# Keys of the windowed block in rows of 16 KB: four heads to a load, and column groups exchanged behind the transposes

## The chip, the cores and the metric

The kernel runs on one core of a Trainium2 chip. The metric is the time of one execution in microseconds (us): the median of the runs, 440.17 us for the kernel before (three runs, 440.09 to 440.18). Beside the runs there is one profiled execution, whose rows are used below.

## The reference, cut to what matters

Two attention blocks, A and B, each decode one token for four sequences. Both have 32 query heads over 8 key and value heads, 8192 cached tokens and 128 numbers to a head. Block A looks at all cached tokens, block B at the last 2048 alone.

```
q = (x @ wq)                                  # x: [4, 1, 512], 32 heads of 128
k, v = cache (A: all 8192 tokens; B: the last W = 2048)   # [4, 8, 8192, 128], bf16
scores = q . k * 128 ** -0.5                  # four query heads share one kv head
o = softmax(scores) @ v
out = concat(o_A @ wo_A, o_B @ wo_B)          # [4, 1, 1024]
```

All of the caches that are looked at are read once: 2 x 67.1 MB for A, 2 x 16.8 MB for B. With the weights the core reads 184.56 MB.

## The kernel before, in words

**Units.** The work is cut into 20 units (the list `units`). Units 0 to 3 belong to B (`P == 1`): one sequence each, all eight heads, 2048 tokens. Units 4 to 19 belong to A (`P == 0`): one sequence and one pair of heads (`gp`) each, 8192 tokens. Each unit has 4 MB of keys and 4 MB of values. `K_sb` and `V_sb` have two slots each, taken in turn by even and odd units (`slot = u % 2`). A slot is 128 partitions of 128 tokens (`NT`) of 256 bytes.

**How a load lies.** `kv_load` (L712) issues the loads, all of them from SyncE's queue (SP). For A, one DMA fills a slot: partition p gets 128 tokens in a row, 32 KB, so that the first 64 partitions hold one head and the last 64 the other. The source pattern is one run of 128 rows. For B, four DMAs (`NSEG`) of 1 MB fill a slot, each with one pair of heads in rows of 32 tokens, 8 KB; the source is walked as 64 rows, 2 heads, 8 KB, and so the two heads alternate from partition to partition.

**Keys.** A unit's keys are transposed in 16 steps (`pe_T`, L270): each step makes four fp32 transposes (two tokens each, bf16 pairs taken as fp32) into one of four PSUM banks (`KT`). VectorE (even steps, L287) or ScalarE (odd steps, L288) copies the bank into `KT_sb`. `pe_S` (L300) then makes eight score matmuls against `RQc`, into `SA` for the first half of the tokens and `SB` for the second (L310). The scores' partition is the column of the transposed key, and it has to agree with the partition of the values in `V_sb`, for `pe_PV` (L317) multiplies the weights with `V_sb` (L326).

**Masks.** A score tile has two heads on its partitions, and for each column one of them counts. `MASK[0]` (A: halves of the partitions) is written by GpSimd's memsets. `MASK[1]` (B: alternating partitions) is made by writing `MK` and spreading it with two DMAs from GpSimd's queue (L563); the first `M1m` waits for them (`("mk", 1)`).

**Order.** TensorE, VectorE and ScalarE run hardware loops over turns of two units, TensorE over all ten turns, with the same instructions in each. In unit u, TensorE does the 16 transposing steps with the scores three steps behind (`LA = 3`), then the values of unit u - 1. SP's queue is in the order of the program: both `wq`, then K of unit 0, and from there K of unit u, V of unit u - 1, and every second unit a piece of `wo`. Each DMA waits until its buffer is free: B's keys by parts (part q waits for transposing step 4q + 3 of unit u - 2), A's keys for the last transposing step of unit u - 2 (u < 6) or for the output of unit u - 3 (`otr`), V for the output of unit u - 2 before it in its slot. The last unit's loads are cut finer (K in two, V in five), and at the end come eight small loads of `wo` (`Wl_sb`).

Of the kernel before, what the change touches and what calls it, by code (L numbers as in the profile page):

```python
# [7 lines left out]
F32 = mybir.dt.float32  # L8
I32 = mybir.dt.int32
ACTF = mybir.ActivationFunctionType  # L10
# [4 lines left out]
def bass_concat_heads__gqa_block_cached__sliding_block_cached__decode_kernel(  # L15
# [34 lines left out]
    NKT = 4  # L50
# [2 lines left out]
    NBK = 4  # L53
    NFILL = 3
    NTH = NT // 2
    X = [A_x, B_x]
    KC = [A_k_cache, B_k_cache]
    VC = [A_v_cache, B_v_cache]
# [13 lines left out]
    with ExitStack() as es:  # L72
        block = es.enter_context(nc.Block())

        def sb(name, shape, dt):
            return es.enter_context(nc.sbuf_tensor(name, shape, dt))
# [4 lines left out]
        def sm(name):  # L81
# [14 lines left out]
        MK = sb("MK", [128, NSEG * C], F32)  # L96
# [28 lines left out]

        names = ["k0", "k1", "kh", "v0", "v1", "vl0", "vl1", "vl2", "vl3", "vl4", "wl0", "wl1", "wl2", "wl3", "wl4", "wl5", "wl6", "wl7", "x0", "x1", "w0", "w1", "wo",
                 "out0", "out1", "out2", "Tq", "Td", "Ta", "S", "PV", "Ed", "Ea", "Eq", "vs", "sub", "exp", "otr", "otp",
                 "ocp", "Ef", "fin0", "fin1", "ar1", "SM", "msk", "pset", "setup", "pm0", "pm1", "oc", "ocB", "mk0", "mk", "mka", "perm", "rq"]
        sems = {n: sm("s_" + n) for n in names}

        K_sbf = K_sb.bitcast(F32)
# [123 lines left out]
        def pe_filler(n):  # L255
# [8 lines left out]
                return ins  # L264
            op("pe", fn, waits=[("F", p) if jobs[p]["turn"] is not None else None])

        def pe_T(u, k):
            eng = "dve" if k % 2 == 0 else "act"
            idx = tjob_idx[(u, k)] = new_job("T", eng)
            tj = u * NJ + k  # L270
            bkf = kbank(idx)
            bk = bkf.bitcast(BF16)
            slot = u % 2

            def fn(pe):
                ins = None
                for pi in range(4):
                    t0 = k * 8 + 2 * pi
                    ins = pe.transpose(out=bkf[:, pi * 128:(pi + 1) * 128],  # L279
                                       in_=K_sbf[:, slot, t0:t0 + 2, :].rearrange("p t d -> p (t d)"),  # L280
                                       identity=identf[:, :])
                return ins
            op("pe", fn, waits=[("K", u) if k == 0 else ("KH", u) if k == NJ // 2 and u % 2 == 1 else None, bankfree(idx)], inc=("T", idx))

            def efn(e):
                if eng == "dve":
                    return e.tensor_copy(out=KT_sb.bitcast(I32)[:, tj % NKT, :], in_=bkf.bitcast(I32)[:, :])  # L287
                return e.activation(out=KT_sb[:, tj % NKT, :], in_=bk[:, :], func=ACTF.Copy)  # L288
            return dict(eng=eng, fn=efn, waits=[("T", idx)], inc=("E", idx))

        def pool_rq(u):
# [8 lines left out]
        def pe_S(u, k):  # L300
            tj = u * NJ + k
            stb = SA[u % 2] if k < NJ // 2 else SB
            ktv = KT_sb[:, tj % NKT, :].rearrange("p (i k e) -> p i k e", i=4, e=2)

            def fn(pe):
                ins = None
                for pi in range(4):
                    t = k * 8 + 2 * pi
# [109 lines left out]
        def dve_addmask(u):  # L418
            n, P = ncol(u), units[u]["P"]

            def fn(dve):
                return dve.tensor_tensor(out=M1m[:, 0:n], in0=M1[:, 0:n] if P == 1 else M1c[:, :], in1=MASK[P][:, 0:n], op=AluOpType.add)  # L422
            return dict(eng="dve", fn=fn, waits=[("max", u, 1) if P == 1 else ("maxc", u)] + ([("mk", 1), ("mka",)] if u == 0 else []), inc=("pm", u, 0))

        def pool_ar1(u):
            n = ncol(u)
# [81 lines left out]
            return dict(eng="pool", fn=lambda pool: pool.tensor_copy(out=OTp[:, :, :], in_=OT_sb[:, P, q, :, :]), waits=w, inc=("otp", tn))  # L508

        def pool_mask0(pool):  # L510
            mkv = MK[:, :].rearrange("p (g s h) -> p g s h", g=NSEG, s=2)
            pool.memset(mkv[0:64, :, 0, :], 0.0)
            pool.memset(mkv[0:64, :, 1, :], -BIG)
            pool.memset(mkv[64:128, :, 0, :], -BIG)
            return pool.memset(mkv[64:128, :, 1, :], 0.0)
        op("pool", pool_mask0, inc=("mk0",))

        def pool_mask1(pool):
# [4 lines left out]
        op("pool", pool_mask1, inc=("mka",))  # L523

        def pool_setup0(pool):
            pool.memset(dummy[:, :], 0.0)
# [8 lines left out]
        op("pool", pool_setup0, waits=[("mk0",), ("mka",)], inc=("pset",))  # L535
# [21 lines left out]
        for sh in range(2):  # L557
            m0 = MASK[1][:, :]
            pstm = m0.ap[0][0]
            dst_ap = bass.AP(tensor=m0.tensor, offset=m0.offset + sh * pstm, ap=[[2 * pstm, 64], [1, NSEG * C]])  # L560

            def mfn(pool, dst_ap=dst_ap, sh=sh):
                return pool.dma_start(out=dst_ap, in_=MK[64 * sh:64 * sh + 64, :])  # L563
            op("pool", mfn, waits=[("mk0",)], inc=("mk", sh))

        def dma(dst, src):
            def fn(e):
                return e.dma_start(out=dst, in_=src)  # L568
            return fn
# [140 lines left out]
        def kv_load(kind, u):  # L710
            un = units[u]
            cache = (KC if kind == "K" else VC)[un["P"]]  # L712
            buf = K_sb if kind == "K" else V_sb
            slot = u % 2
            if kind == "K" and slot == 1 and u < L:
                op("sp", lambda sp: sp.sem_inc(sems["kh"], 16), bump=(sems["kh"], 16, ("KH", u)))
            if un["P"] == 1:
                for q in range(NSEG):
                    base = cache[un["b"], 2 * q, SK - W:SK, :]
                    src = bass.AP(tensor=base.tensor, offset=base.offset, ap=[[TS * DH, 64], [SK * DH, 2], [1, TS * DH]])  # L720
                    if kind == "K":
                        w = [("T", tjob_idx[(u - 2, 4 * q + 3)])] if u >= 2 else []
                    else:
                        w = [("otr", u - 2)] if u >= 2 else [("T", tjob_idx[(1, 1)])] if u else [("T", qp_idx[(1, NQP - 1)])]
                    op("sp", dma(buf[:, slot, q * TS:(q + 1) * TS, :], src), waits=w, inc=(kind if q == NSEG - 1 else kind + "h", u, q))
# [12 lines left out]
            sem = sem_of((kind, u))  # L738
            op("sp", lambda sp: sp.sem_inc(sem, 48), waits=w, bump=(sem, 48, None))
# [28 lines left out]

        def full(key):
            if key[0] in ("K", "V") and len(key) == 2:  # L770
                return (key[0], key[1], NSEG - 1 if units[key[1]]["P"] == 1 else 0)
# [163 lines left out]
```

## Time and profile before

| what | value |
|---|---|
| median of the runs | 440.17 us |
| profiled execution: time, span | 439.76 us, 437.9 us |
| TensorE busy | 363.9 us, 83% of the span |
| VectorE, ScalarE, GpSimd busy | 209.5, 193.3, 29.1 us |
| DMA queue of SP | 12400 packets, 184.56 MB, 99.2% of 16 engines' span |
| HBM read over the span | 421 GB/s |
| mean granted TensorE clock | 0.969 |
| key copies: VectorE L287, ScalarE L288 | 690 ns, 1025 ns each, 160 of each |

The span is the time between the first and the last record of the core; 1.9 us of the profiled execution's time lie around it, and it is 0.4 us under the median. A DMA is issued by an engine's queue, and its rows are moved as packets by the core's 16 DMA engines; the profile counts the packets by queue and gives the mean share of the 16 engines that were busy. KB is 1024 bytes, MB a million.

### The profile page before, as it was taken

To read this page: it belongs to the slowest core of one execution; us is meant where nothing else is said; L and a number is where in the kernel's file an instruction comes from. 1 tells how busy PE (TensorE), PEld (TensorE's weight loads), DVE (VectorE), ACT (ScalarE), POOL (GpSimd) and SP (SyncE) were. 2 spreads that over 40 slices of the span, in tenths; PEclk is the share of its full clock that TensorE was granted. 3 is DMA by queue.
4 is the path that set the end of the run, shared out by engine and by line. 5 is a ranking of instruction groups with operands and counts; after the bars stand their busy time and mean duration, and the time that the engine had idled before them with its cause. 6 is when DMAs were issued, how large, how long until landed. Compare 5 with 4: busy or idle time off the path is not lost.

```text
span 437.9 us, 15510 instructions
## 1 busy us (share of the span) xinstructions
PE 363.9 (83%) x7174; PEld 336.5 (77%) x7184; DVE 209.5 (48%) x404; ACT 193.3 (44%) x217; POOL 29.1 (7%) x96
## 2 busy tenths in 40 slices
PE   0078898998998959896989598969878895989986
PEld 0068897997997959795979588968868795979975
DVE  0004455664565634463456247625644563556641
ACT  1033473563653625372635264534534361635630
POOL 7110000000000000000000000000100000000000
PEclk9999999999999997999899699989998999999999
DMA  8999999999999999999999999999999999999996
GB/s 336 431 412 418 419 419 419 421 445 406 450 431 431 417 445 431 434 428 431 434 434 428 432 434 431 428 434 431 406 456 431 431 428 434 431 431 410 446 407 253
DMA packets 12500, 184.75 MB, mean 422 GB/s; under 512 B 1428, under 2 KB 2504, under 8 KB 2760
## 3 DMA queue, kind: packets, MB, share of 16 engines
q1 hardware_dynamic: 12400, 184.56, 99.2%
q8 instruction: 8, 0.13, 0.1%
q14 instruction: 4, 0.03, 0.0%
q0 software_dynamic: 64, 0.02, 0.0%
q10 hardware_dynamic: 24, 0.01, 0.0%
HBM read 184.56 MB, written 0.01 MB: 421 GB/s over the span
## 4 chain that ended last, share of the span: by engine, by line
PE 51%; DMA 43%; issue 2%; DVE 1%; SPq 1%; PEld 1%; PEldq 0%
DMA K_sb<-in_A_k_cache_dram 29%; PE KT L279 25%; PE OT L326 10%; DMA K_sb<-in_B_k_cache_dram 7%; DMA V_sb<-in_A_v_cache_dram 7%; PE SB L310 4%; PE SA L310 4%; PE KT L384 4%; SPq L568 1%; PE SA L338 1%; DVE oacc L392 1%; PE KT L326 1%; PEld OT L326 1%; PE KT L262 0%; DVE OS L489 0%
## 5 line engine op out<-in xcount | busy, mean ns | idle before, releaser
L279 PE MATMUL KT<-identf,K_sb 128*128 128x128 f32 x1280 | 206.2, 294 | 44.0 <-DMA K_sb<-in_A_k_cache_dram 33.0
L288 ACT ACTIVATE KT_sb<-KT 128x1024 bf16<-128x1024 bf16 x160 | 163.4, 1025 | 121.1 <-PE KT L279 121.1
L279 PEld LDWEIGHTS KT<-identf,K_sb 128*128 128x128 f32 x1280 | 146.2, 148 | 49.4 <-DMA K_sb<-in_A_k_cache_dram 34.2
L287 DVE COPY KT_sb<-KT 128x512 int32<-128x512 int32 x160 | 110.5, 690 | 131.2 <-PE KT L279 129.9
L326 PE MATMUL OT<-PT,V_sb 128*128 128x64 bf16 x2560 | 78.1, 193 | 2.5 <-issue 1.4
L326 PEld LDWEIGHTS OT<-PT,V_sb 128*128 128x128 bf16 x2560 | 75.9, 98 | 2.7 <-issue 1.5
L457 ACT ACTIVATE PT<-Dt 128x512 bf16<-128x512 f32 x40 | 24.6, 632 | 84.1 <-DVE Dt L446 84.1
L310 PEld LDWEIGHTS SA<-RQc,KT_sb 128*128 128x128 bf16 x1280 | 56.7, 98 | 2.3
L310 PEld LDWEIGHTS SB<-RQc,KT_sb 128*128 128x128 bf16 x1280 | 51.1, 97 | 7.9 <-issue 4.4
L310 PE MATMUL SA<-RQc,KT_sb 128*128 128x16 bf16 x1280 | 56.2, 170 | 0.0
L310 PE MATMUL SB<-RQc,KT_sb 128*128 128x16 bf16 x1280 | 52.8, 170 | 0.0
L408 DVE TENSOR_REDUCE M<-SB 128x8 f32<-128x512 f32 (+1 forms) x20 | 13.8, 692 | 49.9 <-PE SB L310 49.9
L429 POOL PARTITION_ALL_REDUCE MB<-M1m x20 | 7.7, 387 | 333.3 <-DVE M1m L422 333.3
L384 PE MATMUL KT<-Wo_sb,OL 128*4 128x512 bf16 x80 | 18.9, 379 | 0.0
L200 PE MATMUL KT<-ident,x_sb 4*128 4x4 bf16 x8 | 0.6, 170 | 21.1 <-POOL identf L540 21.1
L200 PEld LDWEIGHTS KT<-ident,x_sb 4*128 4x128 bf16 x8 | 0.4, 113 | 21.3 <-issue 21.3
L464 DVE TENSOR_REDUCE LB<-SA 128x8 f32<-128x512 f32 (+1 forms) x20 | 13.7, 684 | 2.8 <-PE SA L338 2.8
L446 DVE TENSOR_TENSOR Dt<-SA,MBm 128x512 f32<-128x512 f32 x20 | 13.8, 692 | 0.7
L355 DVE TENSOR_TENSOR ORx<-KT,MSK 32x1024 bf16<-32x1024 bf16 x10 | 12.1, 1211 | 3.7 <-PE KT L350 3.7
L408 DVE TENSOR_REDUCE M<-SA 128x8 f32<-128x512 f32 (+1 forms) x20 | 13.6, 681 | 0.0
L446 DVE TENSOR_TENSOR Dt<-SB,MBm 128x512 f32<-128x512 f32 x20 | 13.6, 681 | 0.0
L338 PE MATMUL SA<-PT,onesb 128*128 128x128 bf16 x168 | 12.7, 218 | 0.0
(74 smaller groups left out, 119.7 us busy)
## 6 DMA issues: line engine op xcount, KB each, us to landing
K_sb<-in_A_k_cache_dram SPq DMA_DIRECT2D x15, 4096.0 KB, 22.6
V_sb<-in_A_v_cache_dram SPq DMA_DIRECT2D x15, 4096.0 KB, 30.6
K_sb<-in_B_k_cache_dram SPq DMA_DIRECT2D x16, 1024.0 KB, 22.0
V_sb<-in_B_v_cache_dram SPq DMA_DIRECT2D x16, 1024.0 KB, 18.4
V_sb<-in_B_wq_dram SPq DMA_DIRECT2D x1, 4096.0 KB, 12.5
V_sb<-in_A_wq_dram SPq DMA_DIRECT2D x1, 4096.0 KB, 22.0
Wo_sb<-in_B_wo_dram SPq DMA_DIRECT2D x4, 1024.0 KB, 11.9
K_sb<-in_A_k_cache_dram SPq DMA_DIRECT2D x2, 2048.0 KB, 18.9
```

The lines of the kernel that those rows point to most:

```text
L279: ins = pe.transpose(out=bkf[:, pi * 128:(pi + 1) * 128], in_=K_sbf[:, slot, t0:t0 + 2, :].rearrange("p t d -> p (t d)"), identity=identf[ ...
L287: return e.tensor_copy(out=KT_sb.bitcast(I32)[:, tj % NKT, :], in_=bkf.bitcast(I32)[:, :])
L288: return e.activation(out=KT_sb[:, tj % NKT, :], in_=bk[:, :], func=ACTF.Copy)
L310: ins = pe.matmul(out=stb[:, t % NTH * C:(t % NTH + 2) * C], lhsT=ktv[:, pi, :, e], rhs=RQc[:, u % 2, t // TS, e, :], start=(e == 0), stop ...
L326: ins = pe.matmul(out=otb[:, s * NW:s * NW + w], lhsT=V_sb[:, slot, t, :], rhs=PT[:, slot, t * C:t * C + w], start=(j == 0), stop=(j == n ...
L338: ins = pe.matmul(out=SA[u % 2][:, s * NM:(s + 1) * NM], lhsT=onesb[:, :], rhs=PT[:, u % 2, c0:c0 + NM], start=(i == 0), stop=(i == n - 1))
L355: return dve.tensor_tensor(out=ORx[:, :, :, :], in0=bk[0:NR, 0:128].rearrange("p (i o r) -> p r o i", o=1, r=C).broadcast_to([NR, C, C, 12 ...
L384: ins = pe.matmul(out=bk[0:Bn, 0:D], lhsT=OL[:, i, :], rhs=Wo_sb[:, i, :], start=(i == 0), stop=(i == C - 1))
L408: return dve.tensor_reduce(out=M1[:, h * n:(h + 1) * n].rearrange("p (s h) -> p s h", h=C), in_=bank[:, :].rearrange("p (s j h) -> p s h j ...
L446: return dve.tensor_tensor(out=Dt[:, h * NTH * C:(h + 1) * NTH * C].rearrange("p (s j h) -> p s j h", s=Sh, h=C), in0=bank[:, :].rearrange ...
L457: return act.activation(out=PT[:, u % 2, a:b], in_=Dt[:, a:b], func=ACTF.Exp, scale=scale)
L464: return dve.tensor_reduce(out=LB[:, 0:n].rearrange("p (s h) -> p s h", h=C), in_=SA[u % 2][:, 0:NSEG * NM].rearrange("p (s j h) -> p s h ...
```

## The change

- **B's keys.** Two DMAs of 2 MB fill a slot instead of four of 1 MB (`NPART["K"] = 2`). A part holds four heads; a row is 64 tokens, 16 KB. The source is walked as 4 heads, 32 rows, 16 KB. Part q waits for transposing step 8q + 7 of unit u - 2.
- **B's values.** Still four DMAs of 1 MB in 8 KB rows; the source is now walked as 2 heads, 64 rows, so the heads lie in halves of the partitions, as in A.
- **A's keys.** Same bytes and row size; the source is now walked as 2, 64, 32 KB: partitions 0 to 63 get the even rows, 64 to 127 the odd ones.
- **Transposes.** All units take other tokens in a step (`tok0`: two from each half of a half slot's segments), and the 128 columns of a transpose are written to PSUM with a step of two fp32 words, which puts A's rows back in order.
- **Copies.** For B the copies out of the bank exchange column groups, so that each score tile holds two heads. VectorE's copy keeps its size with other strides; ScalarE's becomes two of half the size. For A they stay.
- **Masks.** `MASK[1]` now has the halves too and is written by memsets; `MK`, its two DMAs and the wait for them go.

In the program as built, the number of instructions on TensorE, VectorE and GpSimd's computing ones is unchanged; ScalarE has 32 copies more, and SP issues eight loads fewer.

```diff
+    NPART = {"K": 2, "V": NSEG}
...
+        def tok0(k, pi):
+            return NTH * (k // (NJ // 2)) + TS * (pi // 2) + 4 * (k % (NJ // 2)) + 2 * (pi % 2)
+
         def pe_T(u, k):
...
-                    t0 = k * 8 + 2 * pi
-                    ins = pe.transpose(out=bkf[:, pi * 128:(pi + 1) * 128],
+                    t0 = tok0(k, pi)
+                    ins = pe.transpose(out=bkf[:, :].rearrange("p (a j x b) -> p a j b x", a=2, b=2, j=2)[:, pi // 2, pi % 2, :, :],
...
                 if eng == "dve":
-                    return e.tensor_copy(out=KT_sb.bitcast(I32)[:, tj % NKT, :], in_=bkf.bitcast(I32)[:, :])
-                return e.activation(out=KT_sb[:, tj % NKT, :], in_=bk[:, :], func=ACTF.Copy)
+                    dst, sr = KT_sb.bitcast(I32)[:, tj % NKT, :], bkf.bitcast(I32)[:, :]
+                    if units[u]["P"] == 1:
+                        dst, sr = dst.rearrange("p (b y a) -> p b y a", b=2, a=2), sr.rearrange("p (a y b) -> p b y a", a=2, b=2)
+                    return e.tensor_copy(out=dst, in_=sr)
+                dst, sr = KT_sb[:, tj % NKT, :], bk[:, :]
+                if units[u]["P"] == 1:
+                    dst, sr = dst.rearrange("p (b y a e) -> p b y a e", b=2, a=2, e=2), sr.rearrange("p (a y b e) -> p b y a e", a=2, b=2, e=2)
+                    for b in range(2):
+                        ins = e.activation(out=dst[:, b, :, :, :], in_=sr[:, b, :, :, :], func=ACTF.Copy)
+                    return ins
+                return e.activation(out=dst, in_=sr, func=ACTF.Copy)
...
-            mkv = MK[:, :].rearrange("p (g s h) -> p g s h", g=NSEG, s=2)
+            mkv = MASK[1][:, :].rearrange("p (g s h) -> p g s h", g=NSEG, s=2)
...
-                return pool.dma_start(out=dst_ap, in_=MK[64 * sh:64 * sh + 64, :])
-            op("pool", mfn, waits=[("mk0",)], inc=("mk", sh))
...
             if un["P"] == 1:
-                for q in range(NSEG):
-                    base = cache[un["b"], 2 * q, SK - W:SK, :]
-                    src = bass.AP(tensor=base.tensor, offset=base.offset, ap=[[TS * DH, 64], [SK * DH, 2], [1, TS * DH]])
+                base = cache[un["b"], 0, SK - W:SK, :]
+                hw = SK * DH
+                for q in range(NPART[kind]):
                     if kind == "K":
-                        w = [("T", tjob_idx[(u - 2, 4 * q + 3)])] if u >= 2 else []
+                        w = [("T", tjob_idx[(u - 2, 8 * q + 7)])] if u >= 2 else []
+                        ap = [[hw, 4], [2 * TS * DH, 32], [1, 2 * TS * DH]]
+                        dst = buf[:, slot, q * NTH:(q + 1) * NTH, :]
                     else:
...
+                        ap = [[hw, 2], [TS * DH, 64], [1, TS * DH]]
+                        dst = buf[:, slot, q * TS:(q + 1) * TS, :]
+                    src = bass.AP(tensor=base.tensor, offset=base.offset + q * (HKV // NPART[kind]) * hw, ap=ap)
...
-            src = bass.AP(tensor=base.tensor, offset=base.offset, ap=[[NT * DH, 128], [1, NT * DH]])
+            src = bass.AP(tensor=base.tensor, offset=base.offset, ap=[[NT * DH, 2], [2 * NT * DH, 64], [1, NT * DH]] if kind == "K" else [[NT * DH, 128], [1, NT * DH]])
...
             if kind == "K" and u == L:
...
-                    src = bass.AP(tensor=base.tensor, offset=base.offset + t0 * DH, ap=[[NT * DH, 128], [1, NTH * DH]])
+                    src = bass.AP(tensor=base.tensor, offset=base.offset + t0 * DH, ap=[[NT * DH, 2], [2 * NT * DH, 64], [1, NTH * DH]])
```

More of the change, by code (lines that the diff above doesn't have):

```diff
@@ L95, in bass_concat_heads__gqa_block_cached__sliding_block_cached__decode_kernel @@
         permE = sb("permE", [128, 2, 2, 64], BF16)
-        MK = sb("MK", [128, NSEG * C], F32)
         MASK = [sb("MASKA", [128, C], F32), sb("MASKB", [128, NSEG * C], F32)]
@@ L127, in bass_concat_heads__gqa_block_cached__sliding_block_cached__decode_kernel @@
                  "out0", "out1", "out2", "Tq", "Td", "Ta", "S", "PV", "Ed", "Ea", "Eq", "vs", "sub", "exp", "otr", "otp",
-                 "ocp", "Ef", "fin0", "fin1", "ar1", "SM", "msk", "pset", "setup", "pm0", "pm1", "oc", "ocB", "mk0", "mk", "mka", "perm", "rq"]
+                 "ocp", "Ef", "fin0", "fin1", "ar1", "SM", "msk", "pset", "setup", "pm0", "pm1", "oc", "ocB", "mk0", "mka", "perm", "rq"]
         sems = {n: sm("s_" + n) for n in names}
@@ L307, in fn @@
                 for pi in range(4):
-                    t = k * 8 + 2 * pi
+                    t = tok0(k, pi)
                     for e in range(2):
@@ L422, in fn @@
                 return dve.tensor_tensor(out=M1m[:, 0:n], in0=M1[:, 0:n] if P == 1 else M1c[:, :], in1=MASK[P][:, 0:n], op=AluOpType.add)
-            return dict(eng="dve", fn=fn, waits=[("max", u, 1) if P == 1 else ("maxc", u)] + ([("mk", 1), ("mka",)] if u == 0 else []), inc=("pm", u, 0))
+            return dict(eng="dve", fn=fn, waits=[("max", u, 1) if P == 1 else ("maxc", u)] + ([("mka",)] if u == 0 else []), inc=("pm", u, 0))
         def pool_ar1(u):
@@ L522, in pool_mask1 @@
             return pool.memset(MASK[0][64:128, REP:C], 0.0)
-        op("pool", pool_mask1, inc=("mka",))
+        op("pool", pool_mask1, waits=[("mk0",)], inc=("mka",))
         def pool_setup0(pool):
@@ L534, in pool_setup0 @@
             return pool.memset(Wo_sb[:, :, :], 0.0)
-        op("pool", pool_setup0, waits=[("mk0",), ("mka",)], inc=("pset",))
+        op("pool", pool_setup0, waits=[("mka",)], inc=("pset",))
         def pool_setup1(pool):
@@ L556, in bass_concat_heads__gqa_block_cached__sliding_block_cached__decode_kernel @@
         op("dve", dve_msk, waits=[("setup",)], inc=("msk",))
[L557 to L562, printed above, removed]
-                return pool.dma_start(out=dst_ap, in_=MK[64 * sh:64 * sh + 64, :])
-            op("pool", mfn, waits=[("mk0",)], inc=("mk", sh))
         def dma(dst, src):
@@ L717, in kv_load @@
             if un["P"] == 1:
-                for q in range(NSEG):
-                    base = cache[un["b"], 2 * q, SK - W:SK, :]
-                    src = bass.AP(tensor=base.tensor, offset=base.offset, ap=[[TS * DH, 64], [SK * DH, 2], [1, TS * DH]])
+                base = cache[un["b"], 0, SK - W:SK, :]
+                hw = SK * DH
+                for q in range(NPART[kind]):
                     if kind == "K":
-                        w = [("T", tjob_idx[(u - 2, 4 * q + 3)])] if u >= 2 else []
+                        w = [("T", tjob_idx[(u - 2, 8 * q + 7)])] if u >= 2 else []
+                        ap = [[hw, 4], [2 * TS * DH, 32], [1, 2 * TS * DH]]
+                        dst = buf[:, slot, q * NTH:(q + 1) * NTH, :]
                     else:
                         w = [("otr", u - 2)] if u >= 2 else [("T", tjob_idx[(1, 1)])] if u else [("T", qp_idx[(1, NQP - 1)])]
-                    op("sp", dma(buf[:, slot, q * TS:(q + 1) * TS, :], src), waits=w, inc=(kind if q == NSEG - 1 else kind + "h", u, q))
+                        ap = [[hw, 2], [TS * DH, 64], [1, TS * DH]]
+                        dst = buf[:, slot, q * TS:(q + 1) * TS, :]
+                    src = bass.AP(tensor=base.tensor, offset=base.offset + q * (HKV // NPART[kind]) * hw, ap=ap)
+                    op("sp", dma(dst, src), waits=w, inc=(kind if q == NPART[kind] - 1 else kind + "h", u, q))
                 return
@@ L736, in kv_load @@
                 return
-            src = bass.AP(tensor=base.tensor, offset=base.offset, ap=[[NT * DH, 128], [1, NT * DH]])
+            src = bass.AP(tensor=base.tensor, offset=base.offset, ap=[[NT * DH, 2], [2 * NT * DH, 64], [1, NT * DH]] if kind == "K" else [[NT * DH, 128], [1, NT * DH]])
             sem = sem_of((kind, u))
-            op("sp", lambda sp: sp.sem_inc(sem, 48), waits=w, bump=(sem, 48, None))
+            bump = 16 * (NPART[kind] - 1)
+            op("sp", lambda sp: sp.sem_inc(sem, bump), waits=w, bump=(sem, bump, None))
             if kind == "K" and u == L:
@@ L770, in full @@
             if key[0] in ("K", "V") and len(key) == 2:
-                return (key[0], key[1], NSEG - 1 if units[key[1]]["P"] == 1 else 0)
+                return (key[0], key[1], NPART[key[0]] - 1 if units[key[1]]["P"] == 1 else 0)
             if key[0] == "F":
```

## The prediction

> **What bounds the kernel now.** I read the page's slices first, then the DMA queues and the issues, then the waits and a table of windows.
>
> ```profile
> PE   0078898998998959896989598969878895989986
> DMA  8999999999999999999999999999999999999996
> GB/s 336 431 412 418 419 419 419 421 445 406 450 431 431 417 445 431 434 428 431 434 434 428 432 434 431 428 434 431 406 456 431 431 428 434 431 431 410 446 407 253
> ```
>
> The DMA row stands at 9 from the second slice to the last but one; TensorE dips where it waits. The windows give the rates by stage:
>
> ```profile
> 44.00:55.00 11.00, 9.58 (x236) 9.10 (x236) 5.11 (x9) 4.89 (x6) 0.70 (x2) 1.00 1.01 419
> 230.00:270.00 40.00, 33.73 (x652) 31.35 (x652) 20.26 (x40) 17.53 (x20) 1.81 (x7) 0.91 1.00 431
> ```
>
> B's 8 KB rows run at 419 GB/s over 16 engines, 26.2 GB/s an engine; A's 32 KB rows at 431, 26.9 an engine. The last two columns are the DMA share and GB/s: all sixteen engines are busy in both, so the engines are the bound. TensorE's waits confirm it for the A stage:
>
> ```profile
> PEld KT L279 <- DMA K_sb<-in_A_k_cache_dram: 34.2, 10, 5.4
> ```
>
> A unit takes 8.39 MB / 431 GB/s = 19.5 us to load; TensorE needs about 17.5 (two units from 89.45 to 124.40 us in its timeline).
>
> The next rows decide my forecast. They are the queues of SP (q1) and ScalarE (q10) and the issues on them:
>
> ```profile
> q1 hardware_dynamic: 12400, 184.56, 99.2%
> ...
> q10 hardware_dynamic: 24, 0.01, 0.0%
> ```
>
> ```profile
> K_sb<-in_A_k_cache_dram SPq DMA_DIRECT2D x15, 4096.0 KB, 22.6
> V_sb<-in_A_v_cache_dram SPq DMA_DIRECT2D x15, 4096.0 KB, 30.6
> K_sb<-in_B_k_cache_dram SPq DMA_DIRECT2D x16, 1024.0 KB, 22.0
> V_sb<-in_B_v_cache_dram SPq DMA_DIRECT2D x16, 1024.0 KB, 18.4
> ...
> x_sb<-in_B_x_dram ACTq DMA_DIRECT2D x1, 4.0 KB
> x_sb<-in_A_x_dram ACTq DMA_DIRECT2D x1, 4.0 KB
> ...
> out_dram<-osb ACTq DMA_DIRECT2D x1, 2.0 KB
> ```
>
> Count packets. q10 carried three DMAs of four rows: 12 row packets. It shows 24, so each DMA left four more, one completion for each engine that served it. SP issued 88 DMAs: 86 of 128 rows and two of four. Rows: 86 x 128 + 8 = 11016; 12400 - 11016 = 1384 = 86 x 16 + 2 x 4. So a large DMA was served by 16 engines and one whose pattern starts with a count of 4 by four. Of the large ones, B's sources start with a count of 64 (64, 2, 8 KB) and all others with 128.
>
> **The change: the loads.** The new sources start with other counts: 4 for B's keys (4, 32, 16 KB), 2 for B's values (2, 64, 8 KB), 2 for A's keys (2, 64, 32 KB). If the engines that serve a DMA follow the first count of its source, as for the four-row DMAs, B's keys run on four engines, B's values and A's keys on two. If they follow the number of rows, all stay on sixteen. The trace has no long DMA with a small first count, so these are the two ends. A second hint: the three-level sources of B are not treated as a plain run of 128 rows when they are issued:
>
> ```profile
> 55.68 2.48 SPq L568 DMA_DIRECT2D V_sb<-in_B_v_cache_dram  x4
> ...
> 124.76 0.33 SPq L568 DMA_DIRECT2D K_sb<-in_A_k_cache_dram  x1
> ```
>
> 0.62 us an issue for three levels against 0.33 for two: the queue works on the levels, not on a merged list of rows. I take the first end: the only rows with a first count under sixteen got exactly that many engines.
>
> [...]
>
> **The sum at that end.** The four engines of q10's DMAs are not named in the trace; I assume that each DMA starts from the same first engine, so that two engines get a share of everything. Their bytes, each:
> - A's keys: 15 x 4096 KB + 2 x 2048 KB = 67.11 MB on two: 33.55 MB
> - B's values: 16.78 MB on two: 8.39 MB
> - B's keys: 16.78 MB on four: 4.19 MB
> - all else (V of A, `wq`, `wo`): 184.56 - 100.66 = 83.9 MB on sixteen: 5.24 MB
>
> Together 51.38 MB, against 184.56 / 16 = 11.53 MB now. At stage rates: 33.55 / 26.98 (mean of the six 40 us windows of the A stage, 431.7 GB/s) = 1243.7 us; 8.39 / 26.2 = 320.2; 4.19 at 26.6, midway since 16 KB rows lie between, 157.7; 5.24, nine tenths in 32 KB rows, 194.9. Sum 1916.5. By q1's row instead (99.2% of 437.9 us for 11.53 MB, 37.66 us/MB) it is 1935. I take the middle, 1926. No row tells the price of an engine when fourteen others idle; the page's slices bound it. At 450 GB/s / 16 = 28.1 an engine it is 1827, at 406 / 16 = 25.4 it is 2025.
>
> Do the two engines ever run dry? SP's order keeps them fed. K of unit u waits for the output of unit u - 3, which comes some 17.5 us after K of unit u - 2 landed; K of unit u - 1 is then queued already and takes 4096 KB / 2 / 26.98 = 78 us. In the B stage the shortest cover is K of unit 2: it waits for step 7 of unit 0, while K of unit 1 (39 us on four engines) and V of unit 0 (80 us on two) are queued ahead. So they do not run dry.
>
> Ends: the first window's DMA share of 0.84 over 11 us is 1.8 us of start; after the last wait for `Wl_sb` (435.4 us) 2.5 us remain. Span 1926 + 4.3 = 1930; 1.9 us lie around it (439.76 against 437.9) and the median is 0.4 above the profiled execution: 1933 us.
>
> **The other edits, hidden under these loads.** A unit of A then lasts 78 + 9.7 (V) + 1.2 (`wo`) = 89 us with 17.5 us of TensorE work.
> - ScalarE's copies in B: two of 512 elements by L457's 632 ns, 1264 instead of 1025, eight a unit: +1.9 us on 9.5 busy. VectorE's strided copies: L408 reads PSUM with a stride at 692 ns, as fast as the straight copy's 690: nothing.
> - Strided transposes: 1280 of 294 ns with no strided write in the trace; between nothing and a doubling. Each unit has 71 us of cover.
> - Coarser waits of B's key parts, four steps later (2.7 us): queued behind 39 us.
> - Eight issues and two mask DMAs fewer; the mask wait was not among the listed waits. Nothing.
>
> If the sixteen engines stayed, the cover is what TensorE has now, 2.0 us a unit in A (19.5 - 17.5), and in B SP's lead of more than 5 us.
>
> **Rivals.**
> - *All sixteen engines stay* (the other side). Then only row size counts: B's keys, 16.78 MB at 419 GB/s, 40.0 us now; in 16 KB rows at 425 (midway), 39.5; eight completions and 64 mask packets fewer add perhaps 0.2. About -0.8 us: 439.4, on the edge of 0.2% (0.88 us), which is about what a measurement of this kernel can tell from no change. For it: four heads and two halves still make 128 rows, and B's (64, 2) source got 16. Against: q10's packets. It decides if q1 counts 16 completions for each new load. Chance 0.08.
> - *The engines are few but taken in turn.* Each DMA gets a fresh pair, and two K loads run side by side. A K slot is then refilled in 78 + 17.5 us, two slots side by side: 48 us a unit, 16 units 764; about 100 before them and 25 after: 890 us. For it: nothing names the engines. Against: nothing in the queue rows shows a rotation. Chance 0.03.
> - *Sixteen engines, but TensorE becomes the bound.* The transposes write to PSUM with a gap. In the chain four take 0.49 us, 123 ns each; 64 a unit. From 31 ns more on each, the 2.0 us of slack are gone; doubled, a unit takes 25.4 and 16 units add 94 us: 533 us. Chance 0.03. [...]
>
> **How the numbers follow.** Few engines, the same ones: 0.86, 1933 us, between 1834 and 2032 by the slices' rates (1827 and 2025 plus 6.6). That holds more than eight in ten, so it is the range. Slower 0.86 + 0.03 + 0.03 = 0.92; the sixteen-engine rival is split between faster and same, 0.04 each.
>
> **What would show it.** q1 at 9992 rows (78 x 128 + 8) plus completions: 8 x 4 + 16 x 2 + 17 x 2 + 37 x 16 + 2 x 4 = 698, together 10690 packets; with sixteen engines 9992 + 78 x 16 + 8 = 11248. A DMA share near 434 / 1930, 0.22, and 96 GB/s. About 155 us from issue to landing for A's keys (two K loads and a V, less the 17.5 us until the issue). TensorE waiting for A's keys some 70 us a unit. ScalarE's halves at 632 ns, transposes at 294 ns or more, both without effect. The prediction is wrong if the DMA row stays at 9, or if the bytes spread over changing engines, which a share well over 0.22 would show.

## The result and the profile after

The changed kernel takes 2119.99 us (median of six runs, 2107.65 to 2147.59), the kernel before 440.0 us beside it. The ratio is 4.812, with an interval of 4.790 to 4.833. The forecast was 1933 us with a range of 1834 to 2032: slower, as forecast, for the reason that was forecast, but 187 us more, and outside the range. The profiled execution took 2107.65 us, with a span of 2105.8 us.

First the queues of the changed kernel (queue, packets, MB, share of 16 engines) and the line on memory under them:

```profile
q1 hardware_dynamic: 10690, 184.56, 25.8%
...
q10 hardware_dynamic: 24, 0.01, 0.0%
...
HBM read 184.56 MB, written 0.01 MB: 88 GB/s over the span
```

10690 is to the packet the number that stands in the prediction for two, two and four engines, and the shares of busy engines agree: 0.25 of the sixteen from 30 to 40 us, where B's keys load, and 0.12 from 1060 to 1090 us, where A's keys load alone (the windows are below). But the share is 25.8% where 22% was forecast, and the rate 88 GB/s where it was 96. The prediction had named a share well over 0.22 as a sign of changing engines; it does not mean that here, as the packets show below. Put together, an engine that is busy moves 88 / (0.258 x 16) = 21.3 GB/s; before it was 421 / (0.992 x 16) = 26.5. The engines are few, and those that work are slow as well.

The slices of the span for the changed kernel:

```profile
PE   1321201210210302122021303030303022030313
DMA  5212121111141314132512313311413131322162
GB/s 195 91 74 71 73 71 70 53 55 53 54 114 54 134 54 110 59 126 94 136 50 68 116 54 134 118 49 55 126 54 113 71 117 58 108 119 69 51 162 76
```

Many slices of the A stage read 53 to 55 GB/s: two engines at 27 each, the full rate (A's 431 GB/s before are 26.9 an engine). The slices between them, over 100 GB/s, are those with a load on sixteen engines. The first slices after `wq`, where B's keys and values are loaded on four and two engines, stand at 70 to 91.

The costliest groups (count, then busy us and mean ns of one, then idle time before them):

```profile
L282 PE MATMUL KT<-identf,K_sb 128*128 128x128 f32 x1280 | 234.2, 325 | 1415.2 <-DMA K_sb<-in_A_k_cache_dram 1267.9
...
L293 DVE COPY KT_sb<-KT 128x512 int32<-128x512 int32 x160 | 110.5, 690 | 1528.8 <-PE KT L282 1527.5
...
L298 ACT ACTIVATE KT_sb<-KT 128x512 bf16<-128x512 bf16 x64 | 34.7, 594 | 302.0 <-PE KT L282 302.0
```

TensorE's transposes wait 1267.9 us for A's keys. Its list of waits has 17 of them (total us, count, longest us):

```profile
PE KT L282 <- DMA K_sb<-in_A_k_cache_dram: 1267.9, 17, 87.2
...
PE OT L338 <- DMA V_sb<-in_B_v_cache_dram: 262.3, 4, 71.6
...
PE KT L282 <- DMA K_sb<-in_B_k_cache_dram: 147.1, 4, 56.9
```

A wait for A's keys takes 1267.9 / 17 = 74.6 us in the mean (the longest 87.2), where some 70 were forecast for a unit. The profile page gives no time from issue to landing for these loads, so the forecast 155 us stay unchecked. The copies are as cheap as was said: VectorE's stay at 690 ns, ScalarE's halves take 594, and both wait for TensorE nearly all the time.

### The profile page after: what moved, and what is told of

It is laid out like the page before. It is cut to its first block, busy times and chain, and to the rows that moved or that the text cites. A ratio compares the mean times of both kernels' runs of the same rounds, so it can differ in the third digit from the quotient of the medians.

```text
span 2105.8 us, 15531 instructions
## 1 busy us (share of the span) xinstructions
PE 400.9 (19%) x7174; PEld 373.1 (18%) x7184; DVE 209.6 (10%) x404; ACT 195.7 (9%) x249; POOL 27.8 (1%) x94
## 3 DMA queue, kind: packets, MB, share of 16 engines
q1 hardware_dynamic: 10690, 184.56, 25.8%
## 4 chain that ended last, share of the span: by engine, by line
another core or an unknown queue 80%; PE 19%; issue 1%; POOL 0%; ACT 0%; DVE 0%; POOLq 0%
PE KT L282 10%; PE OT L338 4%; PE SB L322 1%; PE SA L322 1%; PE KT L396 1%; PE SA L350 0%; PE KT L223 0%; PE KT L262 0%; PE KT L338 0%; POOL Wo_sb L546 0%; PE KT L380 0%; ACT KT_sb L298 0%; POOL PT L545 0%; PE KT L362 0%
## 5 line engine op out<-in xcount | busy, mean ns | idle before, releaser
L282 PE MATMUL KT<-identf,K_sb 128*128 128x128 f32 x1280 | 234.2, 325 | 1415.2 <-DMA K_sb<-in_A_k_cache_dram 1267.9
L282 PEld LDWEIGHTS KT<-identf,K_sb 128*128 128x128 f32 x1280 | 172.1, 167 | 1419.6 <-DMA K_sb<-in_A_k_cache_dram 1269.9
L300 ACT ACTIVATE KT_sb<-KT 128x1024 bf16<-128x1024 bf16 x128 | 131.1, 1024 | 1487.4 <-PE KT L282 1487.4
L338 PE MATMUL OT<-PT,V_sb 128*128 128x64 bf16 x2560 | 85.5, 199 | 263.3 <-DMA V_sb<-in_B_v_cache_dram 262.3
L338 PEld LDWEIGHTS OT<-PT,V_sb 128*128 128x128 bf16 x2560 | 83.3, 102 | 264.0 <-DMA V_sb<-in_B_v_cache_dram 262.6
L298 ACT ACTIVATE KT_sb<-KT 128x512 bf16<-128x512 bf16 x64 | 34.7, 594 | 302.0 <-PE KT L282 302.0
```

The source lines that it names most:

```text
L282: ins = pe.transpose(out=bkf[:, :].rearrange("p (a j x b) -> p a j b x", a=2, b=2, j=2)[:, pi // 2, pi % 2, :, :], in_=K_sbf[:, slot, t0:t ...
L298: ins = e.activation(out=dst[:, b, :, :, :], in_=sr[:, b, :, :, :], func=ACTF.Copy)
L300: return e.activation(out=dst, in_=sr, func=ACTF.Copy)
L338: ins = pe.matmul(out=otb[:, s * NW:s * NW + w], lhsT=V_sb[:, slot, t, :], rhs=PT[:, slot, t * C:t * C + w], start=(j == 0), stop=(j == n ...
```

## The experiments

Each edit is shown against the kernel named with it. Where neither an interval nor a median is given, the time is that of one run.

### Is it the number of engines, and is it all?

**All loads on sixteen engines** (edit to the changed kernel: each head of B has a DMA of its own, 32 rows of keys or 64 of values; A's keys come in two DMAs of 64 rows).

```
-  src = AP(ap=[[hw, 4], [2*TS*DH, 32], [1, 2*TS*DH]])            # B's keys; values likewise
+  for h in range(heads): src = AP(offset=off + h*hw, ap=[[run, rows], [1, run]])   # to partitions h*rows ...
-  src = AP(ap=[[NT*DH, 2], [2*NT*DH, 64], [1, NT*DH]])           # A's keys
+  for x in range(2): src = AP(offset=x*NT*DH, ap=[[2*NT*DH, 64], [1, NT*DH]])      # to partitions 64x ...
```

> The change with its three new sources cut at their first count: one DMA for each head of B's keys (32 rows) and values (64 rows), one for each parity of A's rows (64 rows). Every byte lands where it does in the changed kernel; transposes, copies and masks are those of the changed kernel. Theory (few engines are the whole loss): every load is served by 16 engines, SP's queue shows 9992 + 131 x 16 + 2 x 4 + 64 x 0 = about 12100 packets, the DMA share is back near 0.99, and the time is 438.8 to 440.2 us (439.4 by the row sizes alone). Rival (the strided transposes or the halved copies cost by themselves): above 445 us, with TensorE and not the DMA engines busy through the A stage.

Measured: 761.48 us (median of six, which differ widely: 702.67 to 856.23). That is four fifths of the way back (1358 of 1680 us), and still far from 440, the fastest run too. Neither expectation came true: the DMA engines, and not TensorE, are busy throughout. The slices and the queue of this kernel say why the number of engines is not enough:

```profile
DMA  9999999999999999999999988989898989998992
...
q1 hardware_dynamic: 12160, 184.56, 94.7%
```

All sixteen are busy, and yet the mean is 241 GB/s (page): 241 / (0.947 x 16) = 15.9 GB/s for a busy engine. A busy engine and a fast engine are two things.

**A's keys alone on sixteen**, then **B's loads alone** (the edits above, one at a time).

> The changed kernel with A's keys alone cut into two DMAs of 64 rows; B's keys stay on a first count of 4 and B's values on 2. Theory: two engines carry 67.11/16 + 8.39 + 4.19 + 5.24 = 22.0 MB, at 26.7 GB/s 825 us, with the slow key packets of the B stage (four engines took up to 1.2 us for 16 KB) some 30 more: 830 to 880 us. SP's queue: the DMAs on few engines leave 4 or 2 completions each. Rival (only A's loads are served by few engines): near 440 us.

> The changed kernel with B's keys and values cut into DMAs of 32 and 64 rows; A's keys stay on a first count of 2. Theory: two engines carry 33.55 + 1.05 + 1.05 + 5.24 = 40.9 MB, at 26.9 GB/s 1520 us, and 90 to 150 us more for the stretches in which all sixteen engines start on the values together and a 32 KB packet takes up to 2.4 us: 1600 to 1690 us. The losses of this run and of the run with B alone on few engines should add up to the whole loss (1680 us) within 60 us. Rival (a pair of engines is slower all the time): 32 KB packets above 1.3 us also where two engines work alone.

Measured: 1152.63 and 1748.79 us, both above what was expected. A's keys on two engines are the larger part, as the bytes of the sum have it (33.55 of 51.38 MB on the two engines), but the two losses, 1152.63 - 440 = 713 and 1748.79 - 440 = 1309, add to 2022 where the whole is 1680. The cuts themselves cost time (with all loads cut, 321 us were left), so the parts can't be read off cleanly.

**A's values on eight engines** (edit to the kernel before: the same bytes and row size, other order).

```
-  ap=[[NT * DH, 128], [1, NT * DH]]
+  ap=[[NT * DH, 8], [8 * NT * DH, 16], [1, NT * DH]]   # A's values
```

> The kernel before, with nothing changed but the source of A's values, walked as 8, 16, 32 KB with other rows to other partitions (so the weights meet other tokens' values, which leaves the result aside). Theory (the first count sets the engines): eight engines carry 62.9/8 + 121.7/16 = 15.5 MB, at 26.9 GB/s 575 and with the ends 582 us, more where packets are slow; SP's queue shows 12400 - 15 x 8 = 12280 packets. Rival (the number of rows sets the engines): 440 us and 12400 packets. Rival (only counts of 2 and 4 fall short): 440 us.

Measured: 975.71 us, and 12280 packets on q1, which is 15 x 8 under the 12400 of before. The first count decides the number of engines here too, in a load that is otherwise untouched. But 975.71 is far above the 582 us of the sum for eight engines: the 32 KB packets took 2234 ns in the mean, against 1217 ns in the A stage of the kernel before.

**A's values on two engines too** (edit to the changed kernel: the values get the pattern of the keys).

> The changed kernel with A's values on two engines too (walked as 2, 64, 32 KB, which puts other rows to other partitions, so the result is left aside). From unit 5 on no load but wo's small pieces runs on more than two engines. Theory (the forecast's rate failed only where full loads run beside the pair): 32 KB packets at 1.21 us throughout the A stage, the pair's bytes 51.38 + 62.9 x (1/2 - 1/16) = 78.9 MB, 2930 us at 27.0 GB/s and some 40 more for the slow key packets of the B stage, the wo pieces and the ends: 2950 to 3000 us. Rival (a pair is slow by itself for a part of the time): the excess over the bytes grows with them, 3150 to 3250 us.

Measured: 2997.24 us, as expected. Its slices:

```profile
GB/s 160 86 73 65 73 54 54 53 54 54 54 65 54 54 54 65 54 54 54 65 54 54 54 66 54 54 53 59 60 54 54 65 53 54 54 54 65 53 87 64
```

In the A stage they stay at 53 or 54 GB/s, apart from some at 59 to 66, and 32 KB packets take 1225 ns. Two engines keep their full rate in a kernel in which no full load of 4 MB runs beside them.

### Why are busy engines slow?

**B's keys on four engines, but other partitions** (edit to the changed kernel: each part in four DMAs, each to 32 neighbouring partitions; still four engines, by the packets: 10786, which is 24 DMAs more with four completions each).

```
-  ap = [[hw, 4], [2*TS*DH, 32], [1, 2*TS*DH]]; dst = buf[:, slot, q*NTH:(q+1)*NTH, :]
+  ap = [[hw, 4], [2*TS*DH, 8], [1, 2*TS*DH]]; dst = buf[32*j:32*j+32, slot, g*NTH:(g+1)*NTH, :]
```

> The changed kernel with each part of B's keys in four DMAs: 4 heads, 8 rows, 16 KB, to 32 neighbouring partitions (other rows to other partitions, so the scores meet other tokens and the result is left aside). [...] Rival (rows 2 MB apart collide in memory): 57 to 67 GB/s as in the changed kernel. Total 2040 to 2110 us.

Measured: 2069.58 us, 38 us under the changed kernel's profiled execution, which is the fastest of its six runs. The windows (the last three columns: granted clock, DMA share, GB/s), of the changed kernel first:

```profile
30.00:40.00 10.00, 0.22 (x2) 0.00 (x0) 0.00 (x0) 0.76 (x2) 0.00 (x0) 1.00 0.25 57
40.00:50.00 10.00, 0.00 (x0) 0.00 (x0) 0.00 (x0) 0.00 (x0) 0.00 (x0) 1.00 0.25 64
```

and of the kernel with four DMAs:

```profile
30.00:40.00 10.00, 1.44 (x42) 1.09 (x39) 0.00 (x0) 1.15 (x4) 0.00 (x0) 1.00 0.26 106
40.00:50.00 10.00, 0.00 (x0) 0.00 (x0) 0.00 (x0) 0.00 (x0) 0.00 (x0) 1.00 0.24 105
```

Four engines in both (a DMA share of a quarter) move 106 GB/s instead of 57. In the changed kernel each of the four counts of a load goes to a quarter of the partitions; in the other one all four go to 32 neighbours. The two kernels have as many engines at work on the same bytes; they differ in the cut of the loads and in the partitions that each writes. In the changed kernel the rate then climbs, over 67, 79, 88 and 98 to 108 GB/s from 90 to 100 us. No trace names an engine, so why the rate is low and then climbs is not shown.

**Or is it the memory?** (edit to the changed kernel: the four heads of a key load 8 KB closer than 2 MB).

```
-  ap = [[hw, 4], [2*TS*DH, 32], [1, 2*TS*DH]]
+  ap = [[hw - TS*DH, 4], [2*TS*DH, 32], [1, 2*TS*DH]]
```

> The changed kernel with the four heads of a key load of B read 2 MB - 8 KB apart instead of 2 MB (earlier tokens of the other heads are read, so the result is left aside); engines, partitions and sizes stay. [...]

Measured: 2123.25 us, and 64 and 69 GB/s in the two windows above: nearly as slow as the changed kernel (57 and 64). So the even distance of 2 MB does not explain this load: with 8 KB less it did not come near the 106 GB/s in these windows.

**Half loads by themselves** (edit to the kernel before: A's values in two DMAs, to partitions 0 to 63 and 64 to 127; rows in their natural order, sixteen engines each).

> The kernel before with A's values in two DMAs of 64 partitions (natural rows, 32 KB, same places) instead of one of 128. All first counts are 64 or 128, so 16 engines serve each. [...] Rival (slow packets come from few-engine loads running beside full ones): 440 us, for there are none here. Rival (the addresses in memory collide): 440 us, the rows are read in the same order as before.

Measured: 658.82 us. Two windows of this run, one with a load of keys to all 128 partitions, one with half loads:

```profile
310.00:315.00 5.00, 4.89 (x110) 4.77 (x107) 0.07 (x1) 0.00 (x0) 0.00 (x0) 0.64 1.03 442
320.00:332.00 12.00, 8.83 (x110) 8.69 (x111) 3.64 (x6) 4.96 (x5) 0.00 (x0) 0.70 1.00 213
```

442 and 213 GB/s, at a DMA share of 1.0 in both: half loads kept all sixteen engines busy, at half the rate. The half loads cost 219 us here for 62.9 MB; at that price the 100.66 MB cut in the run with all loads on sixteen engines would cost 350 us, and 321 were left there. By this estimate half loads are enough to account for what that run had not won back.

**Sixteen engines, 128 partitions, another walk.** Four edits to the kernel before are to separate the walk from the addresses. The first takes rows 16 apart:

```
+  ap=[[NT * DH, 16], [16 * NT * DH, 8], [1, NT * DH]]        # A's values
```

> The kernel before, with nothing changed but the source of A's values, walked as 16, 8, 32 KB (other rows to other partitions, the result is left aside). Theory on counts: a first count of 16 gives 16 engines, SP's queue at 12400 packets. [...] Rival (the number of engines is all that counts): 440 us.

Measured: 627.17 us, far above the rival's 440, with 12400 packets: sixteen engines. The second was meant to keep the addresses and to change the walk alone:

```
+  ap=[[8 * NT * DH, 16], [NT * DH, 8], [1, NT * DH]]         # A's values
```

> From the kernel before; A's values are walked as 16 blocks of 8 neighbouring rows, each row to the partition it has before: the addresses, the bytes, the 16 engines and the 128 partitions are those of the kernel before, only the pattern has another level. [...]

Measured: 439.9 us, but inconclusive: SP's issue took 0.38 us, as for the plain 128 rows, where the 16 by 8 walk took 0.56, so the two levels may have been merged into one. The third keeps two levels that can't be merged, for there is a gap between them, with near rows, and a fourth makes the far distance uneven:

```
+  ap=[[8 * NT * DH - 4096, 16], [NT * DH, 8], [1, NT * DH]]  # third: near rows
+  ap=[[NT * DH, 16], [16 * NT * DH - 4096, 8], [1, NT * DH]] # fourth: 504 KB apart
```

> From the kernel before; A's values are walked as 16 blocks of 8 neighbouring rows of 32 KB, but the blocks lie 8 KB closer than in the cache (block pitch 248 KB), so that the two levels can't be merged. It therefore reads other numbers of the cache than the reference's, the same count of them. [...]

> From the kernel before; A's values in the 16 by 8 walk that took 627 us, with the 8 rows of an engine 504 KB apart instead of 512 KB. It reads other numbers of the cache than the reference's, the same count of them. If the walk makes the packets slow: 600 to 650 us, as with 512 KB. If the even distance of 512 KB does: about 440 us, or clearly under 600.

Measured: 614.97 and 693.52 us, with issues of 0.55 to 0.56 us in both. The third, in a window of the A stage with keys at full rate and values alternating:

```profile
200.00:300.00 100.00, 68.37 (x1098) 63.32 (x1099) 33.93 (x66) 30.76 (x33) 2.82 (x11) 0.81 1.00 271
```

A DMA share of 1.00 at 271 GB/s, with near rows; 90% of the 32 KB packets of the A stage lie under 2531 ns, and the fast ones are at 1213. The same walk is slow with three sets of addresses (rows 512, 504 and 32 KB apart in the inner count), so the walk is the cause and not the distance of the rows. The same addresses with a walk that stays in two levels were not run. Why the walk is slow is not shown either: no trace names the partitions that an engine writes. The fourth is 66 us slower than the first, with only some of the engines at work at times late in the run; why is not known.

### What does a full load cost beside the pair?

**Sixteen engines that start from rest** (edit to the kernel before: A's keys wait one unit longer, for `otr` of u - 2, so that the engines pause between bursts).

> The kernel before with A's key loads waiting for the output of unit u - 2 instead of u - 3, so that the queues run empty before each pair of loads and all 16 engines start from rest together, as they do for the values in the changed kernel, but with no load on few engines beside them. [...]

Measured: 588.86 us; a burst of keys and values took about 20.5 us and ran at full rate (405 and 416 GB/s in windows over two of them). Sixteen engines that start together were not slow here.

**Values kept apart from the pair** (edit to the changed kernel: A's values also wait for the last step of the unit after).

```
-  w = [("otr", u - 2)] if kind == "V" else ...
+  w = [("otr", u - 2)] + ([("pm", u + 1, 0)] if u < L else []) if kind == "V" else ...
```

> The changed kernel with A's values waiting until the keys of the next unit have landed and been transposed, so that a full load and the keys on two engines no longer run at the same time; engines, patterns, sizes and places stay. Theory (packets slow down only while full loads and the pair's loads run together): 32 KB packets at 1.21 to 1.23 us in the A stage, a values' load done in 10 us by all 16 engines, DMA share x 16 and GB/s giving 26 to 27 GB/s a busy engine there. The wait costs what it saves: 78 + 13 + 10 us a unit, 2080 to 2200 us in all. Rival (full loads are slow after the other engines have rested for 80 us): packets at 2.4 us in half of the values' loads, 2250 us or more.

Measured: 2233.89 us, between the expectation and its rival, since the pair now pauses during the values (105 us between two bursts). The packets decide. Two bursts of values in this kernel:

```profile
703.00:713.00 10.00, 0.00 (x0) 0.00 (x0) 0.79 (x2) 1.23 (x2) 0.00 (x0) 0.56 0.88 377
808.00:821.00 13.00, 1.26 (x24) 1.26 (x25) 1.72 (x5) 1.23 (x2) 0.06 (x1) 0.58 0.95 387
```

and two in the changed kernel, where the pair works on keys meanwhile:

```profile
602.00:621.00 19.00, 6.46 (x128) 6.35 (x128) 0.23 (x1) 0.00 (x0) 0.00 (x0) 0.59 0.94 205
694.00:704.00 10.00, 10.00 (x140) 9.72 (x139) 4.91 (x8) 6.40 (x7) 0.00 (x0) 0.79 0.92 367
```

Apart, each burst takes 10.2 to 10.3 us (12.7 with `wo`). In company fourteen bursts took 10.0 to 21.3 us, 14.3 in the mean. In the 602 us burst all engines are at half rate (205 GB/s at a share of 0.94); in the 694 us burst only the pair is, at 2.45 us a packet.

The changed kernel also has stretches in which only two engines are at work and are slow all the same. Its rows for keys alone and for one such stretch:

```profile
1060.00:1090.00 30.00, 0.00 (x0) 0.00 (x0) 0.00 (x0) 0.00 (x0) 0.00 (x0) 0.50 0.12 54
1389.00:1399.00 10.00, 10.00 (x162) 9.53 (x161) 6.10 (x10) 6.14 (x6) 0.00 (x0) 0.89 0.11 26
```

Two engines move 26 GB/s instead of 54, at 2.4 to 2.5 us a packet. From 1091.6 to 1106.4 us it can be followed packet by packet: after its last key packet each of the two moves its eight rows of the values, the first four or five in 1.21 to 1.22 us each, the rest in 1.9 to 2.6. Neither the run with the values kept apart nor the one with the values on two engines has such stretches. Their reason is open.

**Or is it the memory again?** (edit to the changed kernel: the values' rows 30 KB apart).

> The changed kernel with the rows of A's values read 30 KB apart instead of 32 KB (rows overlap by 2 KB, so the result is left aside); engines, partitions, sizes and order stay. [...]

Measured: 2114.91 us, with bursts of 10 to 22 us as in the changed kernel. So the even distance of the rows is not the cause here either. Why one burst slows all engines and another the pair alone is open.

### What of the edits is left when the engines are not lost?

**Rows of 16 KB on sixteen engines** (edit to the kernel before: B's keys with the 32 rows as the first count, 4 heads inside; `tok0` and the copies to match, in two halves on both engines).

```
-  ap=[[TS * DH, 64], [SK * DH, 2], [1, TS * DH]]
+  ap = [[2 * TS * DH, 32], [hw, 4], [1, 2 * TS * DH]]
```

> The kernel before with B's keys alone in 16 KB rows, four heads to a DMA, but walked as 32 rows, 4 heads, so that the first count is 32 and a DMA covers all 128 partitions; heads alternate from partition to partition as before. A's loads, V's loads, the transposes' writes and the masks stay those of the kernel before; the copies out of the bank exchange the columns of head pairs and token halves, two instructions of half size on VectorE and ScalarE alike. [...] Rival (four heads 2 MB apart are slow to read): 16 KB packets near 1.2 us, 460 to 480 us.

Measured: 440.17 us, a ratio of 1.0008 with an interval of 0.9999 to 1.0017: no difference that can be measured, where the prediction's rival had 16 KB rows gain 0.8 us. The queue and the copies of this kernel:

```profile
q1 hardware_dynamic: 11248, 184.56, 98.9%
```

```profile
L297 ACT ACTIVATE KT_sb<-KT 128x512 bf16<-128x512 bf16 x64 | 34.5, 596 | 18.0 <-PE KT L283 18.0
L297 DVE COPY KT_sb<-KT 128x256 int32<-128x256 int32 x64 | 24.2, 419 | 30.4 <-PE KT L283 30.1
```

11248 is the prediction's count for sixteen engines: the first count decides, not the row size and not the number of heads in a load. It is the sound form of the change, and it ties with the kernel before. So two levels do not by themselves make a load slow: 32 by 4 kept the full rate, and 16 by 8 (615 to 694 us) did not. What tells the two walks apart is not shown.

**Transposes with a step in PSUM** (edit to the kernel before: the transposes' output written with a step of two, nothing else).

```
-  out=bkf[:, pi * 128:(pi + 1) * 128]
+  out=bkf[:, :].rearrange("p (a j x b) -> p a j b x", a=2, b=2, j=2)[:, pi // 2, pi % 2, :, :]
```

> The kernel before with one edit: the transposes write their 128 columns to PSUM with a step of two fp32 words, as in the changed kernel. Loads stay; the scores' columns are exchanged, so that scores meet other values (the result is left aside). Theory (a strided write costs nothing): 439.7 to 440.2 us, the chain's four transposes at 0.49 us. Rival (strided writes slow the transposes): TensorE becomes the bound in the A stage from 31 ns more for each; doubled 533 us.

Measured: 439.8 us, a ratio of 1.0004 with an interval of 0.9995 to 1.0013. From its groups by line:

```profile
L279 PE MATMUL KT<-identf,K_sb 128*128 128x128 f32 x1280 | 208.7, 297 | 41.8 <-DMA K_sb<-in_A_k_cache_dram 31.0 <-issue 6.9 <-DMA K_sb<-in_B_k_cache_dram 2.5
```

297 ns against 294 without the step (granted clock 0.957 and 0.969): 3 ns more, a tenth of the 31 ns from which the prediction's rival has TensorE become the bound.

## Why the prediction was right, and where it was wrong

- **Which engines: right.** The count of packets (10690) is exact, and 12280 and 11248 in the experiments follow from the same rule. The step from DMAs of four rows to loads of 4 MB held. The second hint, that the queue works on levels and not on a merged list of rows, did not hold for every walk: 16 by 8 over neighbouring rows took 0.38 us to issue without a gap, like a plain run, and 0.55 to 0.56 with one.
- **The two engines never run dry: right.** In the packets of the A stage practically no moment has fewer than two engines active; 81% of the time there are just two, 14% of it sixteen, and four are at work for 0.2%, where a fresh pair for each load would often show four. That each DMA starts from the same first engine was an assumption; no trace names an engine, but two at work for most of the time fit it. The rival with a changing pair is dead, and so are the two with all sixteen engines.
- **The bytes of the two engines, 51.38 MB: stands.** Nothing in the runs speaks against it, and the run with the values on two engines as well, whose whole time follows from bytes on a pair, came out within its 2950 to 3000.
- **The rate of the two engines: the term that failed.** The sum took 26.7 GB/s (51.38 MB in 1926 us). Measured over the span less the ends it is 51.38 MB / (2105.8 - 4.3 us) = 24.4 GB/s. The bound failed with it: 406 / 16 = 25.4 came from slices of the kernel before, where every large load ran on all sixteen engines, and no such slice can hold what the change makes, few engines on a load and full loads beside a pair. (The upper bound was misread too: the fastest slice shows 456 GB/s and not 450. It did not matter.) The prediction said itself that "No row tells the price of an engine when fourteen others idle"; it then bounded that price by rows which all lie on one side of it. The runs show the price: 2.45 us instead of 1.21 for a 32 KB packet of the pair beside a full load, and 57 GB/s instead of 106 for B's keys at their start.
- **Where the 187 us lie.** B's keys: 38 us, by the run with four DMAs (against the profiled execution; a single run, but the packets agree: 16 KB packets took 968 us of engine time in the changed kernel and 831 in that run, which is 34 us for each of four engines). A: in the chain of waits the long waits for keys begin at 805.73 us and, eleven units later, at 1896.46, so a unit takes 99.2 us where the sum had 89. In a burst of 14.3 us the pair at half rate loses about 7. The stretches in which the pair alone is slow cost each engine 20 us over the eleven units, about 2 each. The load of `wo`, every second unit, takes another 5 us on all engines beside the pair, which costs it some 1 us a unit by an estimate from half rate. Ten us by 16 units and the 38 make about 200, more than the 175 that the profiled execution lies above the sum, so the account closes to some 25 us and no better.
- **The edits beside the loads: right.** ScalarE's halves (594 ns, forecast 632) and VectorE's strided copies (690) are as cheap as forecast. In kernels on sixteen engines, where there is little cover, halved copies with the coarser waits and the strided transposes (297 ns for 294) each tie with the kernel before. VectorE's strided copy in one piece was not run in such a kernel at full rate.
- **The gain of longer rows, in the rival with sixteen engines:** -0.8 us was given; the sound form shows 1.0008 with an interval of 0.9999 to 1.0017. In that interval at most 0.04 us of gain is left.

## What to carry to other kernels

Before a load's source pattern is given another order, look at its first count: here counts of 2, 4 and 8 got two, four and eight engines, and 16, 32, 64 and 128 got sixteen; the completions in the queue's packet count show how many there were. Sixteen engines were not enough for the full rate here: one plain run over all 128 partitions kept it (442 GB/s in a window, where half loads ran at 213), and so did 32 by 4 (440.17 us); 16 by 8 did not (615 to 694 us). So measure a walk before it is used. When a forecast rests on the rate of an engine, ask whether the rows that bound it hold the new way of working at all; if not, the far end of the range lies beyond the slowest slice; here packets of the pair beside a full load fell to half rate (2.45 us for 1.21), and half loads as well (213 GB/s for 442).

## What the runs showed that was not expected

- An issue can hold SP for most of a unit. Of the fourteen 4 MB loads of A's values behind the pair's keys, in SP's timeline of the changed kernel (start us, length us), eleven took 70 to 85 us to issue and three 12 to 19, where before an issue took 0.38. Why is not shown:

```profile
712.98 1.77 SPq L571 DMA_DIRECT2D K_sb<-in_A_k_cache_dram  x1
714.85 85.30 SPq L571 DMA_DIRECT2D V_sb<-in_A_v_cache_dram  x1
```

- The granted clock of TensorE fell to 0.611 in the mean, though TensorE was busy for only 19% of the span; transposes took 325 ns instead of 294. In the kernel before, at 0.969, it was busy for 83%. Nothing waited for it here.
- A share of busy DMA engines says nothing of their rate: 1.00 to 1.03 stood beside 442, 271 and 213 GB/s.
